# SyncE's wait for the output, inside the block or behind its closing barrier

## The chip, the cores and the metric

The kernel runs on one core of one Trainium2 chip. A time is the device time of one execution in microseconds (us). The profile adds the span, from the first to the last instruction of the program, and the clock that TensorE was granted. All profile times below count from the start of the span.

## The reference

One decode step of a layer with attention and a gated feed-forward network in parallel, for 4 sequences of one token each (model width 512, 32 query heads, 8 key/value heads of 128, feed-forward width 1792). Attention sees the last 4096 of 16384 cached positions. All data are bf16.

```python
xn = layernorm(x)                                   # x is A_x, (4, 1, 512)
q  = (xn @ wq) as 32 heads of 128
k, v = the last W = 4096 positions of the caches, each KV head for 4 query heads
p  = softmax(q k^T * 128 ** -0.5)
a  = (p v) @ wo
f  = (silu(xn @ w_gate) * (xn @ w_up)) @ w_down
out = x + a + f                                     # (4, 1, 512)
```

## The kernel before

The program is written engine by engine in one block (`with nc.Block() as block`, line 171). Each engine has its own list of instructions, and semaphores order them against each other. At the end of the block all five engines meet in a barrier; its instructions are recorded under line 171.

The key and value caches come in 16 steps, each with one KV head of two sequences: 2 MB of keys into one half of `KB` and 2 MB of values into one half of `VB`. SyncE issues all these loads and those of the weights on one queue, in an order written out by hand (lines 231 to 245); before it reloads a buffer it waits for the semaphore that says that TensorE is done with it. For each step TensorE transposes the keys (line 382), VectorE evicts the transposes (line 294), TensorE forms the scores, ScalarE takes the exponential (line 263), and TensorE multiplies by the values. The loop runs 8 times over two steps each. Behind it come the feed-forward network, the head rearrangement and the output projection with `WO` (line 485), which arrives in four pieces.

The tail is what the change touches. The last matmul of the output projection counts `s_acc` up; VectorE then copies the sum from PSUM into `y` (line 349) and counts `s_y` up. The output goes out in two halves of 256 columns, 2 KB each: SyncE issues the first (line 247), ScalarE the second (line 267). Both transfers count the semaphore `d_out` up, 16 for each half, so that 32 means that both have landed. SyncE waits for 32 as its last step in the block (line 248). No other engine waits for `d_out`.

Of the kernel before, what the change touches and what calls it, by code (L numbers as in the profile page):

```python
# [10 lines left out]
def bass_parallel_sum__sliding_block_cached__swiglu_ffn__decode_kernel(  # L11
# [10 lines left out]
    out: bass.AP,  # L22
):
    B, _, D = A_x.shape
    _, HKV, Sk, Dh = A_k_cache.shape
    HQ = A_wq.shape[1] // Dh
    F = B_w_gate.shape[1]
# [84 lines left out]
    def sem(name):  # L112
        return nc.alloc_semaphore(name=name)
# [5 lines left out]
    d_out = sem("d_out")  # L119
# [47 lines left out]
    def kv_ap(cache, d):  # L167
        b0 = d % 2 * 2
        return cache[b0:b0 + 2, d // 2, Sk - W:, :].rearrange("b (q t) d -> q b (t d)", t=NT)

    with nc.Block() as block:
# [40 lines left out]
        @block.sync  # L212
        def _(eng):
            def load_k(d):
                if d >= 2:
                    eng.wait_ge(s_tr, 2 * NG * (d - 1))
                eng.dma_start(KB[:, d % 2 * KVN:(d % 2 + 1) * KVN], kv_ap(A_k_cache, d)).then_inc(d_k[d % 2], 16)

            def load_v(d):
                eng.wait_ge(s_pv, d + 1)  # L220
                eng.dma_start(VB[:, d % 2 * KVN:(d % 2 + 1) * KVN], kv_ap(A_v_cache, d)).then_inc(d_v[d % 2], 16)

            def load_v_half(d, h, done):
                a = d % 2 * KVN + h * HKN
                eng.dma_start(VB[:, a:a + HKN], kv_ap(A_v_cache, d)[:, :, h * HKN:(h + 1) * HKN]).then_inc(done, 16)  # L225

            def load_wo(n):
                a, b = WO_CUTS[n], WO_CUTS[n + 1]
                eng.dma_start(WO[:, a:b, :], wo_ap[:, a:b, :]).then_inc(d_wo[n], 16)  # L229

            eng.dma_start(WQ[:], wq_ap).then_inc(d_wq, 16)
            load_k(0)
            load_k(1)
            eng.dma_start(WG[:], wg_ap).then_inc(d_wg, 16)
            eng.dma_start(WU[:], wu_ap).then_inc(d_wu, 16)
            load_v(0)
            for d in range(2, ND):
                load_k(d)
                load_v(d - 1)
            eng.dma_start(WD[:], wd_ap).then_inc(d_wd, 16)  # L240
            eng.wait_ge(s_pv, ND)
            load_v_half(ND - 1, 0, d_v[1])
            load_v_half(ND - 1, 1, d_vz)
            for n in range(len(d_wo)):
                load_wo(n)
            eng.wait_ge(s_y, 1)
            eng.dma_start(out_ap[0], y[0:B, :]).then_inc(d_out, 16)
            eng.wait_ge(d_out, 32)

        @block.scalar  # L250
        def _(eng):
# [234 lines left out]
            last.then_inc(s_acc, 1)  # L486


# [1 line left out]
_INS = ['A_x', 'A_k_cache', 'A_v_cache', 'A_wq', 'A_wo', 'B_x', 'B_w_gate', 'B_w_up', 'B_w_down']  # L490
_OUTS = [((4, 1, 512), 'bfloat16')]
# [23 lines left out]
```

## Time and profile before

| what | value |
|---|---|
| time, three runs | 197.1, 197.37, 197.96 us (median 197.37) |
| time of the profiled execution | 196.87 us |
| its span | 195.1 us |
| granted TensorE clock, mean | 0.991 |
| TensorE busy | 162.7 us (83%) |
| VectorE busy | 114.9 us (59%) |
| ScalarE busy | 16.6 us (9%) |
| data moved by DMA | 81.10 MB, mean 416 GB/s |

The page gives the busy time of each engine and a row of 40 equal slices of the span, with the busy share in tenths. Waits, branches, drains and the issue of a transfer are not counted as busy; they show in the answers for a line, in the timeline and in the waits. A name with a `q` behind it (SPq, ACTq, PEldq) is an engine's sequencer. The duration of a DMA issue is that of the issue, not of the transfer. The profiled execution's time is longer than its span, since something lies ahead of the first instruction and behind the last.

### The profile page before, as it was taken

How to read it: one execution, taken by the hardware profiler on the slowest of the kernel's cores; microseconds unless marked ns; L12 is line 12 of the kernel's file. 1: busy time of each engine (PE TensorE's matmuls, PEld its weight loads, DVE VectorE, ACT ScalarE, POOL GpSimd, SP SyncE). 2: the span in 40 equal slices, each digit the busy share in tenths (PEclk: the TensorE clock that was granted, in tenths of full speed). 3: DMA queues.
4: the chain of work that ended last, by engine and by line, in shares of the span. 5: the costliest groups of instructions: out<-in, count | busy, mean ns of one | idle time of the engine just before them, and what ended most of it. 6: DMA issues, size and time to landing. Idle time of an engine off the chain costs nothing.

```text
span 195.1 us, 7758 instructions
## 1 busy us (share of the span) xinstructions
PE 162.7 (83%) x3466; PEld 140.2 (72%) x3467; DVE 114.9 (59%) x250; ACT 16.6 (9%) x26; POOL 10.3 (5%) x23
## 2 busy tenths in 40 slices
PE   0127999379898989898989898989898989898995
PEld 0113898368887888788878787878787878786752
DVE  1005777237676767676767676767676767675610
ACT  5600101001010101010101010101010101010000
POOL 8930000000000000000000000000000000000000
PEclk9999999789999999999999999999999999999999
DMA  6999999999999999999999999999999999999991
GB/s 222 430 430 430 432 420 437 421 430 430 430 433 430 433 433 430 433 430 433 433 437 430 430 430 430 430 430 430 430 430 430 430 433 433 430 428 420 438 407 68
DMA packets 5934, 81.10 MB, mean 416 GB/s; under 512 B 668, under 2 KB 680, under 8 KB 936
## 3 DMA queue, kind: packets, MB, share of 16 engines
q1 hardware_dynamic: 5912, 81.01, 97.4%
q8 instruction: 5, 0.08, 0.1%
q10 hardware_dynamic: 16, 0.01, 0.0%
q14 instruction: 1, 0.01, 0.0%
HBM read 81.01 MB, written 0.00 MB: 415 GB/s over the span
## 4 chain that ended last, share of the span: by engine, by line
DMA 63%; PE 32%; issue 1%; DVE 1%; SPq 1%; DVEq 0%
DMA kbuf<-in_A_k_cache_dram 48%; PE ps_kt L382 16%; DMA wo_sb<-in_A_wo_dram 9%; PE ps_s L354 8%; DMA wq_sb<-in_A_wq_dram 6%; PE ps_o L354 5%; PE ps_acc L354 2%; PE ps_kt L354 2%; DVE kT L294 1%; SPq L225 1%; DVE kT L282 0%; SPq L229 0%; DVE y_sb L349 0%; DVE qz L285 0%; DVEq L293 0%
## 5 line engine op out<-in xcount | busy, mean ns | idle before, releaser
L294 DVE COPY kT<-ps_kt 128x1024 bf16<-128x1024 bf16 x128 | 79.5, 683 | 25.3 <-PE ps_kt L382 25.3
L382 PE MATMUL ps_kt<-ident,kbuf 128*128 128x128 bf16 x1024 | 62.8, 219 | 10.6 <-DMA kbuf<-in_A_k_cache_dram 10.6
L382 PEld LDWEIGHTS ps_kt<-ident,kbuf 128*128 128x128 bf16 x1024 | 57.3, 98 | 15.8 <-issue 15.7
L354 PE MATMUL ps_o<-p,vbuf 128*128 128x64 bf16 x1120 | 39.2, 195 | 0.0
L354 PEld LDWEIGHTS ps_o<-p,vbuf 128*128 128x128 bf16 x1120 | 36.0, 99 | 1.1
L354 PEld LDWEIGHTS ps_s<-qz,kT 128*128 128x128 bf16 x1024 | 31.7, 98 | 6.7 <-issue 3.6
L354 PE MATMUL ps_s<-qz,kT 128*128 x1024 | 34.9, 192 | 1.3
L299 DVE TENSOR_REDUCE rm<-ps_s 128x8 bf16<-128x512 f32 x17 | 11.8, 692 | 23.7 <-PE ps_s L354 23.7
L263 ACT ACTIVATE p<-ps_s 128x512 bf16<-128x512 f32 x17 | 10.1, 597 | 162.1 <-PE ps_s L354 162.1
L354 PE MATMUL ps_o<-p,ones 128*128 128x128 bf16 (+1 forms) x69 | 7.1, 225 | 4.6 <-DMA vbuf<-in_A_v_cache_dram 3.2
L354 PEld LDWEIGHTS ps_o<-p,ones 128*128 128x128 bf16 x69 | 4.6, 100 | 5.6 <-DMA vbuf<-in_A_v_cache_dram 3.4
L354 PE MATMUL ps_kt<-wq_sb,xnT 128*32 128x512 bf16 x32 | 3.4, 610 | 5.2 <-DMA wq_sb<-in_A_wq_dram 5.2
L359 PE MATMUL ps_acc<-i,xn 4*128 4x4 f32 x4 | 0.6, 254 | 7.4 <-ACT xn L260 7.4
L354 PE MATMUL ps_s<-mkc,mkr 2*128 2x512 bf16 x17 | 6.5, 385 | 0.0
L354 PE MATMUL ps_s<-dg,ones 8*128 8x512 bf16 x17 | 6.5, 385 | 0.0
L354 PEld LDWEIGHTS ps_kt<-wq_sb,xnT 128*32 128x32 bf16 x32 | 1.3, 140 | 6.8 <-issue 6.8
L282 DVE STREAM_TRANSPOSE kT<-ps_kt 128x512 f32<-128x512 f32 x2 | 1.4, 718 | 7.8 <-PE ps_kt L354 7.8
L359 PEld LDWEIGHTS ps_acc<-i,xn 4*128 4x128 f32 x4 | 0.6, 207 | 7.3 <-issue 7.3
L310 DVE TENSOR_REDUCE den<-ps_o 128x8 f32<-128x128 f32 x18 | 4.9, 274 | 1.0 <-PE ps_o L354 1.0
L207 POOL MEMSET vbuf<- 128x6144 f32 x1 | 5.2, 5222 | 0.0
L304 DVE TENSOR_REDUCE m<-ps_acc 8x1 f32<-8x128 f32 x17 | 4.6, 269 | 0.3 <-PE ps_acc L354 0.3
L314 DVE TENSOR_TENSOR oT<-ps_o,den 128x8 f32 (+1 forms) x18 | 3.0, 167 | 2.9 <-issue 2.7
(67 smaller groups left out, 50.0 us busy)
## 6 DMA issues: line engine op xcount, KB each, us to landing
kbuf<-in_A_k_cache_dram SPq DMA_DIRECT2D x16, 2048.0 KB, 12.6
vbuf<-in_A_v_cache_dram SPq DMA_DIRECT2D x15, 2048.0 KB, 11.3
wq_sb<-in_A_wq_dram SPq DMA_DIRECT2D x1, 4096.0 KB, 12.3
vbuf<-in_A_v_cache_dram SPq DMA_DIRECT2D x2, 1024.0 KB, 9.2
wo_sb<-in_A_wo_dram SPq DMA_DIRECT2D x1, 2048.0 KB, 14.4
wg_sb<-in_B_w_gate_dram SPq DMA_DIRECT2D x1, 1792.0 KB, 25.7
wu_sb<-in_B_w_up_dram SPq DMA_DIRECT2D x1, 1792.0 KB, 29.3
wd_sb<-in_B_w_down_dram SPq DMA_DIRECT2D x1, 1792.0 KB, 15.0
```

The costliest lines, as they stand in the source:

```text
L207: eng.memset(VB[:, HKN:].bitcast(FP32), 0.0)
L225: eng.dma_start(VB[:, a:a + HKN], kv_ap(A_v_cache, d)[:, :, h * HKN:(h + 1) * HKN]).then_inc(done, 16)
L263: eng.activation(P[:, d % 2 * PS:d % 2 * PS + SN], ps_S[d % 2][:], ACT.Exp, scale=SCALE).then_inc(s_p, 1)
L282: eng.transpose(qT[:, 512 * n:512 * n + 512], ps_kt[n][:])
L294: eng.tensor_copy(KT[:, u * HKN + 1024 * g:u * HKN + 1024 * (g + 1)], kt_ps[g].rearrange("p a b -> p (a b)")).then_inc(s_ev, 1)
L299: eng.tensor_reduce(RM[:], ps_S[bank][:].rearrange("p (t c) -> p c t", c=C), AX.X, ALU.max).then_inc(s_rm, 1)
L304: eng.tensor_reduce(m8[:], mt_ps, AX.X, ALU.max)
L310: eng.tensor_reduce(den[:], den_ps.rearrange("p (t c) -> p c t", c=C), AX.X, ALU.add)
L314: eng.tensor_tensor(OT[:, 2 * b:2 * b + 2, ds(r * REP, REP)], O_ps.rearrange("p (j h) -> p j h", j=2), den[:].rearrange("p (j h) -> p j h" ...
L354: return eng.matmul(o, l, r, start=start, stop=stop, skip_group_check=True)
L359: last = eng.transpose(xT_ps[:, c * B:(c + 1) * B], xn[:].rearrange("b (p c) -> b c p", c=NC)[:, c, :], I4[:])
L382: last = eng.transpose(kt_ps[g][:, k, :], KB[:, a:a + 128], ident[:])
```

## The change

SyncE's last step in the block, the wait for `d_out` to reach 32, is taken out of the block. The same wait is written behind the end of the block, so that it comes on SyncE's list of instructions after the barrier that closes the block. Nothing else is edited.

```diff
@@ -245,7 +245,6 @@
                 load_wo(n)
             eng.wait_ge(s_y, 1)
             eng.dma_start(out_ap[0], y[0:B, :]).then_inc(d_out, 16)
-            eng.wait_ge(d_out, 32)
 
         @block.scalar
         def _(eng):
@@ -486,6 +485,9 @@
             last.then_inc(s_acc, 1)
 
 
+    nc.sync.wait_ge(d_out, 32)
+
+
 # ---- launch: one core; inputs and outputs as the reference has them ----
```

## The prediction

> **What bounds the kernel now.** I read the page first (span, slices, queues), then the chain of waits, then the end of the timeline, and last the line that closes the block.
>
> ```profile
> span 195.1 us, 7758 instructions
> ...
> DMA  6999999999999999999999999999999999999991
> ...
> q1 hardware_dynamic: 5912, 81.01, 97.4%
> ...
> DMA 63%; PE 32%; issue 1%; DVE 1%; SPq 1%; DVEq 0%
> ```
>
> The kernel is a stream of loads. SyncE's queue (q1) keeps the sixteen DMA engines at work for 97.4% of the span, and in 38 of the 40 slices the DMA digit is 9. Of the chain that ended last, 63% is DMA. An edit that touches no load, no matmul and no eviction can change nothing in those slices. What remains is the last slice, whose DMA digit is 1: there the loads are over and the tail runs one step after another. The timeline of that tail (start, duration, engine, line) is:
>
> ```profile
> 190.66 2.21 PE L354 MATMUL ps_acc<-wo_sb,oP 128*4 128x256 bf16 x32
> ...
> 192.92 0.43 DVE L349 CAST y_sb<-ps_acc 128x256 bf16<-128x256 f32 x1 [5.54 <-PE ps_acc L354]
> 193.37 0.35 SPq L247 DMA_DIRECT2D out_dram<-y_sb  x1
> 193.38 0.28 ACTq L267 DMA_DIRECT2D out_dram<-y_sb  x1
> ```
>
> The last projection ends at 192.87 (190.66 + 2.21), the copy of `y` at 193.35, and the two output halves are issued side by side at 193.37 and 193.38. The issue ends on SyncE at 193.72 (193.37 + 0.35). From there to the end of the span at 195.1 there are 1.4 us, and they are all that this change can reach inside the span.
>
> Those 1.4 us are seen in the instructions of line 171, where the block is opened; its closing barrier is recorded under that line too. The columns are engine, operation, count, duration in ns (min/median/max), and the first and last start in us:
>
> ```profile
> L171 POOLq EVENT_SEMAPHORE  x2: 17/17/17, 195.0 to 195.0; - x2
> L171 POOLq DRAIN  x1: 89/89/89, 11.4 to 11.4; - x1
> L171 PEldq DRAIN  x1: 432/432/432, 192.5 to 192.5; - x1
> L171 DVEq DRAIN  x1: 458/458/458, 192.9 to 192.9; - x1
> L171 ACTq DRAIN  x1: 241/241/241, 193.7 to 193.7; - x1
> L171 SPq COMPARE_BRANCH  x1: 33/33/33, 194.8 to 194.8; - x1
> L171 SPq DRAIN  x1: 13/13/13, 194.9 to 194.9; - x1
> L171 SPq EVENT_SEMAPHORE  x1: 17/17/17, 195.1 to 195.1; - x1
> L171 ACTq EVENT_SEMAPHORE  x1: 17/17/17, 195.1 to 195.1; - x1
> L171 DVEq EVENT_SEMAPHORE  x1: 21/21/21, 195.1 to 195.1; - x1
> L171 PEldq EVENT_SEMAPHORE  x1: 51/51/51, 195.1 to 195.1; - x1
> ```
>
> Each engine drains and reports; GpSimd collects the reports and answers (its two semaphore instructions at 195.0); the other four take the answer at 195.1 and are done. Four engines have drained long before: GpSimd at 11.5, TensorE at 192.9, VectorE at 193.4, ScalarE at 193.9. Only SyncE is late, and the queue's own waits say why:
>
> ```profile
> SPq L171 <- DMA out_dram<-y_sb: 1.0, 1, 1.0
> SPq L171 <- PEq L171: 0.2, 1, 0.2
> ```
>
> SyncE stands 1.0 us before its branch out of the block, until the output has landed (193.72 + 1.0 = 194.7, against the branch's start at 194.8). Only then come drain, barrier and release, with 0.2 us more of waiting inside the barrier. The wait of line 248 is carried by the branch, since line 248 has no instruction of its own. So today's order is: output issued, output landed, barrier. The barrier is last on the path and nothing hides it.
>
> **The change part by part.** Nothing is added or removed in count: one wait on the same semaphore with the same value 32 moves behind the barrier. It is moved past no transfer: the output's own issue (line 247) stands ahead of it in both orders, and ScalarE's half (line 267) is on ScalarE. The start of the output transfers and their landing near 194.8 should therefore stay where they are.
>
> *Term 1, the barrier goes beside the transfer.* SyncE is free at 193.72. Its way into the barrier is today's step from branch to drain, 194.8 to 194.9, so 0.1 to 0.2 us. Its drain takes 13 ns after a wait of 1 us; right behind an output issue the nearest row is ScalarE's drain, which stands behind such an issue itself and takes 241 ns. I take both in full: 193.72 + 0.2 + 0.24 = 194.2 at the latest; at the earliest 193.9, ScalarE's own arrival (193.7 + 0.241). From SyncE's drain to the release it takes 0.2 us today (194.9 to 195.1). The barrier is thus over between 194.1 and 194.4. The transfer that hides it lands at 194.8, so 0.4 to 0.7 us of cover remain. If that cover were gone, the barrier would stand on the path again with its 0.2 us.
>
> *Term 2, what then ends last.* SyncE's wait behind the barrier is released at 194.8 and costs one semaphore instruction of 17 ns. Nothing of the kernel is queued behind it on SyncE and no engine waits for SyncE any more. The last instruction is then at 194.8 instead of 195.1: **0.3 us off the span**, 195.1 to 194.8. The bounds from the row of starts, which are rounded to 0.1, are 0.2 and 0.4.
>
> *Term 3, what lies outside the span.* The profiled execution took 196.87 us with a span of 195.1, so 1.8 us lie outside it and no row shows them. Today five engines leave the kernel together at 195.1. Afterwards four of them leave near 194.2 and SyncE at 194.8. If those 1.8 us hold another meeting of the engines, the part that the four do before it is done early. The nearest row is the kernel's own barrier, where the last arrival costs 0.2 us to the release: an ending like it could get shorter by 0 (if SyncE's own steps carry it) up to about 0.4 (two such meetings). A loss here would need an engine to be later than today, and none is. I take the middle, 0.2, the price of one barrier.
>
> [...]
>
> The sum is 0.3 + 0.2 = 0.5 us. For the profiled execution 196.87 - 0.5 = 196.4. The runs shown have 197.1, 197.37 and 197.96, so the profiled one lies 0.5 under their median; the cut is a fixed one, and from the median it gives 197.37 - 0.5 = **196.9 us**, 0.25% less. The four times spread over 1.1 us, 0.55%, so about 0.5% is what a measurement of this kernel can tell from no change, and this gain lies under it.
>
> **The rivals.**
>
> *The drain holds SyncE until its transfer has landed.* Then the change doesn't do what it says: the drain would end at 194.8, the barrier would follow, and the span would end at 195.0 or 195.1, a gain of 0 to 0.1 (197.3). Against it stands ScalarE's drain: issued at 193.7 right behind an output transfer, over in 241 ns at 193.9, while SyncE was held for the transfers until 194.8. For it stands only that SyncE's own drain was never seen with a transfer in flight. [...] Chance 0.08. The wait could also be put ahead of the barrier again when the program is built; same price, chance 0.03.
>
> *More is hidden than one barrier.* If half of the 1.8 us outside the span is work that each engine does before it meets the others, four engines do it during the output's flight: 0.3 + 0.9 = 1.2 us, 196.2. For it: the four engines would be up to 0.9 us ahead (194.2 against 195.1). Against it: SyncE has to do its own share after 194.8 in any case. Chance 0.14.
>
> *Slower: SyncE has to fetch the code behind the block.* Today SyncE stands 1.0 us at its branch, and the next instruction is there 0.1 us later; a fetch could be hiding in that microsecond of waiting. After the change SyncE runs straight into the barrier, and all five engines would wait for it. The price comes from this row and the wait above:
>
> ```profile
> q8 instruction: 5, 0.08, 0.1%
> ```
>
> Five code packets at 0.1% (0.05 to 0.15%) of 16 x 195.1 us are 0.3 to 0.9 us each, and the way of a small transfer is the 1.0 us of the output: up to 1.9 us. SyncE would drain at 193.72 + 0.2 + 1.9 = 195.8 and be released at 196.0: 0.9 us more than now, 198.3. It decides from the point at which SyncE's drain comes later than today's 194.9, so with a fetch of over 1.0 us. Against it: SyncE's code is short, and its end has long been near when it stands 18.2 us for `y`:
>
> ```profile
> SPq L247 <- DVE y_sb L349: 18.2, 1, 18.2
> ```
>
> Chance 0.05.
>
> **How the numbers follow.** The forecast, a cut of 0.2 to 0.8 us, has 0.70; no gain 0.08 + 0.03; the larger cut 0.14; slower 0.05. The likeliest is 196.9. The low end of the range takes both upper bounds (0.4 + 0.4) from the median, 196.6, and goes on to 196.2 for the larger cut. The high end takes no gain at all, 197.37, and 0.1 for the scatter of the medians: 197.5. Outside lie the slow rival (0.05), a cut of over 1.2 us (0.05), and what the scatter of the runs throws out of either end (0.1). Faster by over 0.5% needs under 196.4: most of the larger cut, 0.11, and of the forecast what scatter brings there, 0.08, so 0.19. Slower by over 0.5% needs 198.4: the upper half of the slow rival and a little scatter, 0.04. The rest, 0.77, is within 0.5%.
>
> **What the profile of the changed kernel would show.** Right: SyncE's drain of the closing barrier starts at 193.7 to 194.0 instead of 194.9, GpSimd's two semaphore instructions at 194.0 to 194.3, the four other engines' last instructions before 194.4, and SyncE's last one alone at 194.8, under a new line behind the block; the wait on the output stands in the queue's own waits with 0.3 to 0.7 us instead of 1.0; the span is 194.8; the two output issues and everything ahead of them are where they were. Step 1 is wrong if SyncE's drain is long and ends with the landing, or if the output lands later than 194.8. Step 3 is wrong if the time outside the span, 1.8 us, stays or grows. The whole is wrong if a gap stands between SyncE's issue and its drain, or if the time moves by more than the last slice can give, 1.4 us.

## The result and the profile after

The median fell from 197.3 us (20 runs) to 196.38 us (20 runs). The ratio of the two is 0.9962, with a 95% interval of 0.9947 to 0.9977: 0.75 us less, between 0.45 and 1.05. (The two medians lie 0.92 us apart, the two means 0.77; the text goes by the ratio.) The change pays, by 0.2 to 0.5 per cent.

The time splits into two parts that scatter very differently. The spans of the 20 runs lie between 194.9 and 196.8 us. In the traces of all twelve kernels of this document the output is issued 0.92 us behind the landing of the last load, so this scatter arises while the loads come in and not in the tail. What lies outside the span (time minus span of the same run) is 1.20 to 1.32 us in every one of them, median 1.27. Before, it was 1.68 to 1.85, median 1.76 (31 runs taken later for comparison). So **0.5 us of the gain lies outside the span**, and there the two ranges do not touch.

The tail of the timeline after (start, duration, engine, line):

```profile
190.76 2.26 PE L353 MATMUL ps_acc<-wo_sb,oP 128*4 128x256 bf16 x32
...
193.06 0.42 DVE L348 CAST y_sb<-ps_acc 128x256 bf16<-128x256 f32 x1 [5.53 <-PE ps_acc L353]
193.51 0.35 SPq L247 DMA_DIRECT2D out_dram<-y_sb  x1
193.52 0.28 ACTq L266 DMA_DIRECT2D out_dram<-y_sb  x1
```

In this execution the output is issued at 193.51, 0.14 us later than in the profiled execution of before. The last load landed 0.14 us later too, so this is the scatter of the loads, and it hides a part of the gain: the spans, 195.1 and 194.9, differ by only 0.2. Distances from the issue or the landing have to be compared, not positions. The instructions of the closing barrier (line 171) and the new line behind the block (line 488):

```profile
L171 POOLq EVENT_SEMAPHORE  x2: 17/17/17, 194.1 to 194.2; - x2
L171 POOLq DRAIN  x1: 89/89/89, 11.4 to 11.4; - x1
L171 PEldq DRAIN  x1: 432/432/432, 192.6 to 192.6; - x1
L171 DVEq DRAIN  x1: 458/458/458, 193.1 to 193.1; - x1
L171 ACTq DRAIN  x1: 242/242/242, 193.8 to 193.8; - x1
L171 SPq DRAIN  x1: 168/168/168, 193.9 to 193.9; - x1
L171 SPq EVENT_SEMAPHORE  x1: 17/17/17, 194.2 to 194.2; - x1
L171 ACTq EVENT_SEMAPHORE  x1: 17/17/17, 194.2 to 194.2; - x1
L171 DVEq EVENT_SEMAPHORE  x1: 21/21/21, 194.2 to 194.2; - x1
L171 PEldq EVENT_SEMAPHORE  x1: 51/51/51, 194.2 to 194.2; - x1
```

```profile
L488 SPq EVENT_SEMAPHORE  x1: 17/17/17, 194.9 to 194.9; - x1
```

```profile
SPq L488 <- DMA out_dram<-y_sb: 0.6, 1, 0.6
SPq L171 <- PEq L171: 0.2, 1, 0.2
```

SyncE's recorded branch is gone from line 171. Its drain starts straight behind the issue (193.9) and takes 168 ns with the transfer under way; the barrier is over at 194.2; SyncE then stands 0.6 us on line 488 until the output has landed, and its one semaphore instruction at 194.9 ends the span. The other four engines left the program 0.6 us before.

Outside the span the page shows nothing, but the trace's record of semaphore updates goes on. There semaphore 2 is updated nine times, twice over. The traces name no engine for a count. The nine counts fit a token that goes from the first engine to the fifth and back, and the text calls them so; the runs with the wait on each engine show for the first five counts which engine is which, and that the last four are the way back was not shown. The first nine, in us from the output's landing (194.744 before, 194.893 after):

```
before    0.640 0.675 0.881 0.925 0.949 | 1.055 1.093 1.127 1.174
after    -0.358 -0.324 -0.118 -0.073 0.151 | 0.195 0.233 0.267 0.315
```

Before, the token starts 0.64 us behind the landing. After, the first four counts come before the output has landed, and only the fifth waits. The token is back (the ninth count) 0.315 us behind the landing instead of 1.174: **0.86 us earlier**, of which 0.37 are in the span (its end lies 0.034 instead of 0.401 behind the landing) and 0.49 outside. The ratio's 0.75, with its interval, agrees. What follows the token in the record is as long as before: 1.14 us to the last of the second nine counts, against 1.15.

### The profile page after: what moved, and what is told of

Its sections match the earlier page's. It is cut to its first block, busy times and chain, and to the rows that moved or that the text cites. A ratio compares the mean times of both kernels' runs of the same rounds, so it can differ in the third digit from the quotient of the medians.

```text
span 194.9 us, 7758 instructions
## 1 busy us (share of the span) xinstructions
PE 164.7 (84%) x3466; PEld 141.7 (73%) x3467; DVE 115.5 (59%) x250; ACT 16.6 (9%) x26; POOL 10.3 (5%) x23
## 4 chain that ended last, share of the span: by engine, by line
DMA 61%; PE 34%; issue 1%; DVE 1%; SPq 1%; DVEq 0%
DMA kbuf<-in_A_k_cache_dram 46%; PE ps_kt L381 18%; DMA wo_sb<-in_A_wo_dram 9%; PE ps_s L353 8%; DMA wq_sb<-in_A_wq_dram 6%; PE ps_o L353 5%; PE ps_kt L353 2%; PE ps_acc L353 2%; DVE kT L293 1%; SPq L225 1%; DVE kT L281 0%; SPq L229 0%; DVE y_sb L348 0%; DVE qz L284 0%; DVEq L292 0%
## 5 line engine op out<-in xcount | busy, mean ns | idle before, releaser
L381 PE MATMUL ps_kt<-ident,kbuf 128*128 128x128 bf16 x1024 | 65.7, 225 | 10.5 <-DMA kbuf<-in_A_k_cache_dram 10.5
L381 PEld LDWEIGHTS ps_kt<-ident,kbuf 128*128 128x128 bf16 x1024 | 60.2, 101 | 15.7 <-issue 15.6
L353 PE MATMUL ps_o<-p,vbuf 128*128 128x64 bf16 x1120 | 38.4, 193 | 0.0
L353 PEld LDWEIGHTS ps_o<-p,vbuf 128*128 128x128 bf16 x1120 | 35.2, 98 | 1.1
```

Source lines behind the costliest of these rows:

```text
L353: return eng.matmul(o, l, r, start=start, stop=stop, skip_group_check=True)
L381: last = eng.transpose(kt_ps[g][:, k, :], KB[:, a:a + 128], ident[:])
```

## The experiments

Each experiment is compared with runs of the kernel before that were taken beside it. Their medians are 197.22 us for the wait on VectorE inside the block and for the waits behind it on TensorE, VectorE and GpSimd, 197.48 for all experiments with further barriers, and 197.37 for the wait on ScalarE and for the drain; so small differences between ratios of different groups mean nothing.

Theory, a supposition from the two traces: (a) a barrier behind the landing costs its full length, ahead of it nothing; (b) behind the program a token passes the engines in a fixed order with SyncE last, so early leavers hide their part of it. The main rival: SyncE's own step was the cost, its branch that carried the wait.

**The wait inside the block, on VectorE.**

```diff
             eng.dma_start(out_ap[0], y[0:B, :]).then_inc(d_out, 16)
-            eng.wait_ge(d_out, 32)
...
             eng.tensor_copy(y[:], ps_acc[:, 0:256]).then_inc(s_y, 1)
+            eng.wait_ge(d_out, 32)
```

The first part is SyncE's, the second VectorE's; what stands between them is left out.

> The wait on the output stays inside the block but is VectorE's last step instead of SyncE's. Theory (the barrier behind the landing is what cost the time, whoever waits): VectorE's drain comes only after the landing, the barrier of 0.2 us is again behind it, the span ends about 0.3 us after the landing, the time outside the span stays at 1.7 to 1.8 us, and the time is within 0.2 us of the kernel before (197.1 to 197.3). Rival (the cost was SyncE's own: a branch that carries the wait, and what follows it on that engine): SyncE is free of it, the time falls as in the changed kernel, to 196.4 to 196.6, with 1.3 us outside the span.

Measured: 197.29 us, ratio 1.0002 (0.9978 to 1.0026), 1.75 us outside the span. Its line 171:

```profile
L171 SPq DRAIN  x1: 168/168/168, 194.5 to 194.5; - x1
L171 DVEq COMPARE_BRANCH  x1: 47/47/47, 195.5 to 195.5; - x1
L171 DVEq DRAIN  x1: 19/19/19, 195.7 to 195.7; - x1
L171 SPq EVENT_SEMAPHORE  x1: 17/17/17, 195.9 to 195.9; - x1
```

SyncE drains at 194.5, early as in the changed kernel, and it helps nothing: VectorE's branch now carries the wait, its drain comes at 195.7, and all are released at 195.9. The span ends 0.47 us behind the landing, not the 0.3 that was expected: VectorE's step from its branch to its drain alone takes 0.21 us. The main rival falls as the explanation of the whole gain. Since VectorE's branch carries the wait here, this run can't tell what such a branch costs on any engine; the last two experiments do.

**The wait behind the block, on each of the other engines.**

```diff
-    nc.sync.wait_ge(d_out, 32)
+    nc.tensor.wait_ge(d_out, 32)
```

The other three runs have `nc.vector`, `nc.gpsimd` and `nc.scalar` in its place.

> The wait stands behind the block's barrier as in the changed kernel, but on TensorE. Theory (behind the program the engines pass a token along in an order in which TensorE is first and SyncE last): the 0.3 us inside the span are gained, but nothing outside, since every later hop has to follow TensorE: 1.6 to 1.8 us outside the span, time 196.9 to 197.0. Rival (what counts is only that four engines leave early, whichever they are): 1.2 to 1.3 us outside the span, time 196.4.

> The wait stands behind the block's barrier, on VectorE. Theory (token order TensorE, ScalarE, GpSimd, VectorE, SyncE): VectorE is next to last, so all but the last hops are hidden: 1.3 to 1.4 us outside the span, time 196.4 to 196.6. Rival (only SyncE's place brings the gain outside the span): 1.7 us outside, time 196.9.

> The wait stands behind the block's barrier, on GpSimd. Theory (GpSimd is third of five in the token order, and the slowest to answer): between the two others, 1.4 to 1.7 us outside the span, time 196.6 to 196.9. Rival (any engine will do): 1.2 to 1.3 us outside, time 196.4.

> The wait stands behind the block's barrier, on ScalarE, second in the token order. GpSimd, third in it, needs about 0.5 us from its leaving to its own hop, which lies beside the wait then; so the hops behind ScalarE follow at 0.04 us each. Theory: one hop better than with the wait on TensorE (1.56 us outside), 1.5 us, time 196.6 to 196.8. Rival (the order is another one): 1.3 us or 1.75.

In all of them the span ends 0.04 to 0.08 us behind the landing, so the 0.3 us inside the span come whoever waits, for instance on TensorE:

```profile
L171 PEldq EVENT_SEMAPHORE  x1: 51/51/51, 194.8 to 194.8; - x1
L488 PEldq EVENT_SEMAPHORE  x1: 51/51/51, 195.5 to 195.5; - x1
```

Outside the span they differ. The counts are in us from the landing; the one that the waiting engine held up is in brackets:

| waits | ratio (95%) | outside, median | first five counts of the token | token back |
|---|---|---|---|---|
| SyncE (the change) | 0.9962 (0.9947 to 0.9977) | 1.27 | -0.358 -0.324 -0.118 -0.073 [0.151] | 0.315 |
| VectorE | 0.9967 (0.9948 to 0.9986) | 1.38 | -0.348 -0.314 -0.107 [0.204] 0.227 | 0.452 |
| ScalarE | 0.9942 (0.9920 to 0.9963) | 1.42 | -0.358 [0.152] 0.190 0.234 0.258 | 0.483 |
| TensorE | 0.9976 (0.9954 to 0.9997) | 1.56 | [0.275] 0.309 0.348 0.391 0.414 | 0.639 |
| GpSimd | 0.9978 (0.9956 to 1.0001) | 1.80 | -0.356 -0.322 [0.578] 0.623 0.646 | 0.871 |

The place of the held count is the engine's place: TensorE first, then ScalarE, GpSimd, VectorE, SyncE. The order of (b) is shown, and "any engine will do" falls. Three sizes outside the span were off. GpSimd was expected at 1.4 to 1.7 and has 1.80: behind its wait it needs 0.54 us from its last instruction of the program to its count (0.56 to 0.57 in the other traces in which its count is the late one), ScalarE and SyncE behind theirs some 0.12, VectorE 0.16, TensorE 0.20. TensorE, expected at 1.6 to 1.8, has 1.56, and ScalarE, expected at 1.5, has 1.42, since GpSimd's half microsecond lay hidden beside the wait there (its count, the third, comes 0.04 us behind the second in both). The times of TensorE (196.68) and ScalarE (196.45) were below what was expected too. The ratios overlap, GpSimd's interval reaches 1, and ScalarE's ratio is even the lowest; that SyncE is the best place is read from the token and the time outside, not from the medians (196.38 and 196.45).

**More barriers ahead of the wait.**

```diff
+    nc.all_engine_barrier()
     nc.sync.wait_ge(d_out, 32)
```

The other two runs have the new line twice and four times.

> The changed kernel with one more barrier of all engines between the block's own and SyncE's wait. Theory (barriers ahead of the wait lie beside the output's flight; SyncE has 0.6 us to spare there, the token behind the program about 0.2 us until it reaches SyncE): a barrier costs about 0.26 us, so the span stays at 0.03 us behind the landing and the time outside the span grows by at most 0.1 to 1.3 to 1.4 us; time 196.3 to 196.6. Rival (each barrier costs its 0.26 us wherever it stands): time 196.7, more span.

> The changed kernel with two more barriers ahead of SyncE's wait, about 0.52 us in all. Theory: SyncE still has its 0.6 us, so the span still ends 0.03 us behind the landing, but the other four leave so late that the token comes to SyncE 0.3 us after SyncE is ready: outside the span 1.5 to 1.6 us, time 196.6 to 196.8. Rival (the gain outside the span is one fixed amount that comes whenever SyncE leaves last): 1.27 outside, time 196.4.

> The changed kernel with four more barriers ahead of SyncE's wait, about 1.04 us in all, more than the output's flight covers. Theory: the last barrier ends about 0.4 us after the landing, where the kernel before ended too; all five engines leave together, 1.75 us outside the span; the time is that of the kernel before, 197.1 to 197.4. Rival (barriers behind the block are hidden or cheap whatever their number): 196.4 to 196.6.

| barriers ahead of the wait | median, ratio (95%) | span's end behind the landing | outside, median |
|---|---|---|---|
| the block's own (the change) | 196.38, 0.9962 (0.9947 to 0.9977) | 0.03 | 1.27 |
| one more | 196.47, 0.9953 (0.9928 to 0.9977) | 0.03 | 1.48 |
| two more | 196.77, 0.9964 (0.9942 to 0.9985) | 0.09 | 1.72 |
| four more | 197.61, 1.0009 (0.9985 to 1.0034) | 0.74 | 1.71 |

SyncE's rows with four more, each barrier on a line of its own:

```profile
L171 SPq EVENT_SEMAPHORE  x1: 17/17/17, 194.3 to 194.3; - x1
L488 SPq EVENT_SEMAPHORE  x1: 17/17/17, 194.6 to 194.6; - x1
L489 SPq EVENT_SEMAPHORE  x1: 17/17/17, 194.9 to 194.9; - x1
L490 SPq EVENT_SEMAPHORE  x1: 17/17/17, 195.3 to 195.3; - x1
L491 SPq EVENT_SEMAPHORE  x1: 17/17/17, 195.6 to 195.6; - x1
L492 SPq EVENT_SEMAPHORE  x1: 17/17/17, 195.7 to 195.7; - x1
```

A barrier costs 0.33 us (194.3 to 195.6 are four of them), not the 0.26 that was expected. Two fit beside the flight of the output and leave the span's end near where it was; with four the fourth ends at 195.6, 0.7 us behind the landing where 0.4 was expected, and the whole gain is gone. The cover of the token is smaller: the first extra barrier already costs 0.2 us outside the span, twice what was expected. GpSimd then leaves only 0.32 us ahead of the landing and its count comes 0.25 us behind it, so that the token reaches SyncE at 0.313 instead of 0.151. The second costs another 0.24 (1.72 outside, where 1.5 to 1.6 was expected), the rest nothing, because by then nobody leaves early enough. The rival of a fixed amount outside the span, which comes whenever SyncE leaves last, had 1.27 for two more barriers; SyncE left last there too, and 1.72 refutes it.

**A barrier behind the wait.**

```diff
     nc.sync.wait_ge(d_out, 32)
+    nc.all_engine_barrier()
```

> The changed kernel with one more barrier of all engines behind SyncE's wait, so that again all five engines leave the program together after the landing. Theory (what counts is that a barrier follows the landing): 0.25 to 0.35 us from the landing to the span's end, 1.75 us outside it, time 197.1 to 197.3, the gain is gone. Rival (the gain came from taking the wait off SyncE's branch out of the block): only the barrier's 0.26 us is added, 1.27 us outside, time 196.7.

Measured: 197.0 us (197.1 to 197.3 was expected), ratio 0.9989 (0.9963 to 1.0016), 1.72 us outside.

```profile
L488 SPq EVENT_SEMAPHORE  x1: 17/17/17, 194.9 to 194.9; - x1
L489 SPq DRAIN  x1: 7/7/7, 195.0 to 195.0; - x1
L489 SPq EVENT_SEMAPHORE  x1: 17/17/17, 195.1 to 195.1; - x1
L489 PEldq EVENT_SEMAPHORE  x1: 51/51/51, 195.1 to 195.1; - x1
```

The wait is off the branch, as in the changed kernel, and still most of the gain is gone: the token is back 1.047 us behind the landing. But it is 0.127 earlier than before (1.174), and the span ends 0.288 behind the landing, not 0.401. About a tenth of a microsecond did belong to SyncE's way out of the block.

**A drain that takes the wait, inside the block.**

```diff
             eng.wait_ge(d_out, 32)
+            eng.drain()
```

> The kernel before with a drain behind SyncE's wait inside the block, so that the drain carries the wait and the branch out of the block follows it free. Theory A (a branch that carries a wait is slow to go on: 0.16 us from its start to the barrier's drain in the kernel before, against 0.06 from a plain wait to the drain where a barrier stood behind the wait): 0.1 us less from the landing to the span's end, 0.3 instead of 0.4; time 197.2. Theory B (any way out of the block behind the wait costs that, the branch being there in both): 0.4 us as before or a little more, time 197.3. Both: 1.75 us outside the span.

Measured: 197.06 us (197.2 was expected), ratio 0.9989 (0.9965 to 1.0013), 1.77 us outside.

```profile
L249 SPq DRAIN  x1: 13/13/13, 194.8 to 194.8; - x1
L171 SPq DRAIN  x1: 7/7/7, 194.9 to 194.9; - x1
L171 SPq EVENT_SEMAPHORE  x1: 17/17/17, 195.1 to 195.1; - x1
```

The drain with the wait starts 0.016 us behind the landing and the barrier's drain 0.067 later; with the wait on the branch that step took 0.163. The span ends 0.298 behind the landing and the token is back at 1.072, 0.10 earlier than before. Theory A holds by the trace, of one execution; the ratio can't tell so small a step from none. The trace records no branch on line 171 here, and none on SyncE in the changed kernel. Whether it is there and takes no time, and why it goes on so slowly behind a wait, stays open.

Leaving the wait out altogether, to see what it still costs, was not tried: in the changed kernel all engines are through the barrier 0.6 us ahead of the landing, and nothing else in the program waits for it.

## Why the prediction was right, and where its size was off

*What can be reached.* Right: the stream of loads is as it was (431 GB/s before and 430 after between 22 and 172 us, the output issued 0.92 us behind the last load's landing in both), and everything happened behind the output's issue.

*Term 1, the barrier beside the transfer.* Right. SyncE's drain took 168 ns, between the 13 and the 241 that bounded it, and the release came 0.4 us behind the issue's end (193.86 to 194.25), at the early end of what was given. The cover left was 0.6 us, inside the forecast 0.4 to 0.7. That a barrier costs 0.2 us was the step from the last arrival alone; a whole one takes 0.33.

*Term 2, 0.3 us off the span.* Right, 0.37 by distance from the landing, against bounds of 0.2 and 0.4. It is two things that the prediction took as one: 0.25 for the barrier, and 0.1 for the branch that carried the wait, which it had put down as a plain way into the barrier.

*Term 3, outside the span.* The mechanism was right, the size was the step that failed: 0.2 was taken, with bounds of 0 and 0.4, and 0.49 was measured. The bounds were made from the kernel's own barrier, where the engines report to one collector (GpSimd, its two instructions at 195.0 between SyncE's drain and the release); the first five counts behind the program come one engine after another, and SyncE's is the fifth, so not a middle part but all four other engines' part was hidden. Before, SyncE's count came 0.55 us behind the end of the span, after, 0.12: that is 0.43 of the 0.49, and the other 0.06 is a shorter step to the sixth count (0.106 and 0.044). The largest piece of what was hidden is GpSimd's half microsecond from its last instruction to its count (0.57 in both traces), which no row of the page shows.

The second round of nine counts takes 0.358 us before and 0.356 after, eight steps of 0.045 us in the mean. Single steps of it take from 0.023 to 0.098 us, and in the first round of before the step to GpSimd's count alone took 0.206 us.

*The sum.* 196.9 was forecast and 196.38 measured, a cut of 0.75 by the ratio (0.45 to 1.05) and of 0.86 by the token, against 0.5. Of the 0.36 that is missing by the token, 0.29 is term 3 and 0.07 term 2. With 0.86 the cut is just above the 0.8 that both upper bounds gave together, and the median lies below their 196.6, in the stretch of the range that was added for the rival of a larger cut. That the number fell inside the range is in that part luck: the room came from a rival and not from the sum. That a gain of 0.25% could not be told from none held for single runs; the interval of 20 against 20 is 0.3% wide and leaves out 1.

*The rivals.* A drain that holds SyncE until its transfer has landed: refuted by the 168 ns: the drain was over at 194.09, 0.8 us ahead of the landing at 194.89, with the output still under way. The wait put ahead of the barrier again: refuted by its row on line 488 behind the barrier's. Half of the time outside being hidden, 0.9 us: GpSimd's half microsecond is such a stretch ahead of its count, so this mechanism was in part what happened, and the measured 0.49 lies between 0.2 and 0.9. A fetch of code: SyncE's drain started 0.06 us behind its issue, so there was none ahead of the barrier, where it would have held all engines.

## What to carry to other kernels

The end of this program was a chain of its own, and what shortened it was the order: issue the output, let every engine pass the closing barrier while the transfer is in flight, and wait for the landing last, on the engine whose count in the ending comes last (here SyncE: 1.27 us outside the span, against 1.38 to 1.80 with the wait on another engine). A barrier behind that wait took most of the gain away (the token back at 1.047 us behind the landing instead of 0.315), and further barriers ahead of it ate into the cover: the first cost 0.2 us outside the span, and with four nothing of the gain was left. To judge such small steps, compare distances from the landing and the time outside the span (1.20 to 1.32 us in the 20 runs), since the load stream's scatter (spans of 194.9 to 196.8 us) drowns them in the total. All this was measured on one kernel, whose output flies for 1.0 us behind its issue.

## What the runs showed of the hardware

GpSimd took 0.54 to 0.57 us from its last instruction of the program to its part in the ending, against 0.12 us for SyncE and ScalarE behind a wait. The branch that carried the wait took 0.16 us from its start to the drain behind it on SyncE (before) and 0.21 on VectorE (the wait in the block on VectorE), the drain that carried it 0.07 on SyncE. Four barriers of all engines in a row took 0.33 us each. In the changed kernel the drain right behind the issue of a transfer took 168 ns on SyncE and 242 on ScalarE, and was over 0.8 us ahead of the landing on both.
